# RWKV attention and a wave mixer on one core: the same tasks in another order, on other engines and banks

## The chip, the core and the metric

The kernel runs on one core of a Trainium2 chip. Five engines work side by side, each through its own list of instructions in order: TensorE (PE, with its weight loads PEld), VectorE (DVE), ScalarE (ACT), GpSimd (POOL) and SyncE (SP), which issues most transfers. The metric is the time of one execution on the device in microseconds (us): lower is better. Three runs of the kernel before gave 139.4, 140.91 and 140.97 us, a median of 140.91.

## What is computed

For batch 4, 8 heads, 768 tokens and head size 48 the first half is a linear recurrence with a decay `w` per channel and a bonus `u` for the present token; the second half mixes tokens and channels:

```python
for t in range(S):
    cur = np.einsum('bhd,bhe->bhde', u[None] * kt, vt)
    y[:, :, t] = np.einsum('bhd,bhde->bhe', rt, state + cur)
    state = w[None, :, :, None] * state + np.einsum('bhd,bhe->bhde', kt, vt)
# x = y with heads joined: (4, 768, 384)
theta = x @ w_theta
zr, zi = x * np.cos(theta), x * np.sin(theta)
u = x + einsum('ts,bsd->btd', w_tok_r, zr) + einsum('ts,bsd->btd', w_tok_i, zi)
out = u + np.maximum(u @ w_ch, 0.0)
```

Inputs and output are float32.

## The kernel before, in words

The 768 tokens of a batch are three groups of 256 tokens, so that there are twelve groups, g0 to g11. For each group `front` loads k, r and v (384 KB each, by SP, lines 436 and 442), multiplies k and r with powers of the decay into `Kw` and `Rw` (lines 551 and 553), turns both with products against an identity (line 487; the copy out of the bank into `KT` or `RT` is line 502 on ACT or 503 on DVE), forms the masked products of k and r (scores, line 601; the masked copy out is `mAT`, line 615, or an ACT copy in line 611 and a multiplication in 617 on DVE or 619 on POOL), the state sums (line 675, then `F`, `T`, `N`, `Sb`, `Sd` in lines 690 to 731), the bonus (`PD` in line 625, `diag` in 642, `dg` in 647, `yd` in 651) and the outputs (lines 751, 764, 780, or 803 and 816), which land in `x`. Then `x` is turned to `xT`, multiplied with `w_theta` (line 839), ACT takes cosine and sine (846, 850) and DVE forms `z` (854). For each batch `mixing` multiplies `z` with the turned token weights `WrT` and `WiT` (line 876, 288 products of 384 columns in all), adds x (`un`, line 889 on DVE, or 886 on ACT and 891 on POOL), turns the sum, multiplies with `w_ch` (line 906) and finishes in line 915 on DVE, or in 912 on ACT and 919 on POOL. The token weights are fetched by six transfers from POOL's queue (line 456), which also convert them, into buffers that later hold other things; each third of them is turned on PE.

Nothing in the program decides the order while it runs. All work is cut into 838 tasks, made in a fixed sequence; a table written out by hand, `ORDER`, gives the sequence in which they are issued, `WAYS` picks for each position one of the engines that the task may run on, `BANKS` gives each group of products its PSUM bank, and `IDLE` names tasks after which PE runs a few products of zeros that nobody reads (line 290, 128x512 each). Each engine then executes its instructions in this sequence, and each waits for what its data need:

```python
for seq in order:
    t = self.tasks[seq]
    way = t.ways[int(ways[seq])]
    if way[0] == PE:
        for tok in t.acq:
            self.bank_of[tok] = int(next(given))
    out = way[-1]()
    for k, n in idle.get(seq, ()):
        unread(k, n, 4)
```

So an instruction whose data are late holds up all that stands behind it on its engine.

Of the kernel before, what the change touches and what calls it, by code (L numbers as in the profile page):

```python
# [27 lines left out]


ORDER = [  # L30
# [46 lines left out]
]  # L77

WAYS = (
    "0000000000000000000000000001000000000000010100000000010000100101001000010100000000011000"  # L80
    "0010012000000000001000000000011000000000000012000000000011000000010000000000000000000000"
    "0000000010000000100100000000000100001000000111100000010010100000100000000000000010010001"
    "1000000001000000000000100100000000000000000000000000000000000000010000000000000000011010"
    "1101100001100000010110110000000000001011011000011000000000000000000000000000000011200000"
    "0000000110100001100011001001000000000001200000000000011000000111100012000100000001200000"
    "0000000000001201101100000000000120110110000110000012011011000000001200101200012120000001"
    "0110000012000000000000101200100012012001000000011000001200000000000000120000111201100000"
    "1000000012000000000000000001201101100001100000120000110000000001112011011000000000001201"
    "1011000000000111201101100001100000000110010110")

BANKS = (
    "0123456701324562704135674127530461542706524316507210431270642067520634705610761234720654"
    "1736504106713526701542765043620752163452316437021323152123756325702705217056302145701414"
    "57142542136074374036124653710465702675143067")

AFTER = []

IDLE = [
    (6, 2, 5), (29, 3, 2), (72, 5, 6), (121, 5, 3), (119, 6, 3), (102, 5, 1), (105, 2, 6),
]  # L100


# [871 lines left out]
```

## Time and profile before

| what | number |
|---|---|
| median of 3 runs | 140.91 us (139.4 to 140.97) |
| the profiled execution's own time | 140.95 us |
| its span, first to last instruction | 139.1 us |
| PE busy | 126.9 us, 91% |
| DVE busy | 114.5 us, 82% |
| ACT busy | 82.3 us, 59% |
| POOL busy | 69.9 us, 50% |
| mean granted TensorE clock | 0.988 |
| moved by DMA | 25.65 MB, 184 GB/s over the span |

In rows of the trace the first number is the start in us and the second how long it took; `L551` is the line of the program; in brackets stands how long the engine was idle just before, and what ended that. Busy time of PE is modelled from overlapping products, so two products of 0.33 us that start 0.16 us apart count once where they overlap. DVE and POOL rows include time in which an instruction has begun and makes no progress.

### The profile page before, as it was taken

Reading aid. Unit: us, or ns where it says so; the run is one execution under the profiler, and the core shown is the slowest. Engines: PE = TensorE matmul, PEld = TensorE weight load, DVE = VectorE, ACT = ScalarE, POOL = GpSimd, SP = SyncE. Lnnn points to the kernel's source line nnn. Section 1 sums busy time; section 2 is a strip of 40 time slices with the busy share of each in tenths; the row PEclk is TensorE's granted clock in tenths of the full one; section 3 lists DMA queues with packets and bytes.
Section 4 is the critical chain, followed back from the end, with each engine's and each line's share of the span. In section 5 each row is a group of like instructions: output and inputs, shape, how many; then the busy total and the mean of one; then the engine's idle time right before and its main releaser. Section 6 shows DMA issues by size and latency. Waiting matters only on the chain.

```text
span 139.1 us, 4476 instructions
## 1 busy us (share of the span) xinstructions
PE 126.9 (91%) x1867; PEld 82.9 (60%) x1867; DVE 114.5 (82%) x211; ACT 82.3 (59%) x160; POOL 69.9 (50%) x68
## 2 busy tenths in 40 slices
PE   6984998869995999999996999999999999999990
PEld 1244575547583787767774666667666665656640
DVE  7199988998989999999999999987794897473191
ACT  3862779959862339987885972686066435810110
POOL 5475629960067093099992009397956426002010
PEclk9999599999999999999999999999999999999999
DMA  4999999999999997999332088899999366365235
GB/s 103 273 261 261 266 211 289 236 249 239 246 227 238 244 188 135 212 221 170 73 114 60 5 216 179 136 265 165 172 299 224 76 184 80 68 226 169 58 125 215
DMA packets 67966, 25.65 MB, mean 184 GB/s; under 512 B 62569, under 2 KB 67946, under 8 KB 67946
## 3 DMA queue, kind: packets, MB, share of 16 engines
q1 hardware_dynamic: 65500, 22.42, 74.2%
q0 software_dynamic: 2432, 2.95, 12.3%
q8 instruction: 14, 0.23, 0.7%
q14 instruction: 6, 0.05, 0.2%
q10 hardware_dynamic: 14, 0.00, 0.0%
HBM read 20.06 MB, written 4.72 MB: 178 GB/s over the span
## 4 chain that ended last, share of the span: by engine, by line
PE 76%; DVE 17%; ACT 3%; issue 1%; DVEq 0%
PE bank L876 32%; PE bank L487 10%; PE bank L906 9%; PE bank L839 8%; PE bank L601 4%; DVE Kw L551 4%; DVE PD L625 3%; DVE mAT L615 3%; PE bank L290 3%; PE bank L675 2%; PE bank L816 2%; PE bank L751 2%; PE bank L764 1%; PE bank L642 1%; PE bank L780 1%
## 5 line engine op out<-in xcount | busy, mean ns | idle before, releaser
L876 PE MATMUL bank<-z,WrT 128*128 128x384 bf16 x144 | 46.9, 327 | 1.1 <-DVE mAT L615 1.1
L876 PE MATMUL bank<-z,WiT 128*128 128x384 bf16 x144 | 46.8, 326 | 0.0
L876 PEld LDWEIGHTS <-WiT 128*128 128x128 bf16 x144 | 14.1, 98 | 9.3 <-issue 1.4
L876 PEld LDWEIGHTS <-WrT 128*128 128x128 bf16 x144 | 14.0, 97 | 8.5 <-ACT WrT L502 0.2
L846 ACT ACTIVATE trig<-bank,pi 128x384 f16<-128x384 f32 x24 | 13.9, 585 | 8.6 <-PE bank L839 8.5
L915 DVE SCALAR_TENSOR_TENSOR fin_all<-bank,uu_all 128x384 f32<-128x384 f32 x23 | 12.3, 553 | 7.2 <-PE bank L906 6.9
L891 POOL TENSOR_TENSOR uu_all<-fin_all,x 128x384 bf16<-128x384 f32 x7 | 7.9, 1122 | 18.5 <-ACT fin_all L886 18.4
L502 ACT ACTIVATE RT<-bank 128x1024 bf16<-128x1024 bf16 x12 | 12.3, 1024 | 6.6 <-PE bank L487 6.5
L615 DVE TENSOR_TENSOR mAT<-bank,mask 128x512 bf16<-128x512 f32 x23 | 15.2, 682 | 1.0 <-PE bank L601 1.0
L611 ACT ACTIVATE mAT<-bank 128x512 bf16<-128x512 f32 x18 | 10.4, 601 | 9.2 <-PE bank L601 9.1
L839 PE MATMUL bank<-Wth,xT 128*128 128x384 bf16 x72 | 14.8, 327 | 0.2 <-DVE xT L503 0.2
L906 PE MATMUL bank<-Wch,uu_all 128*128 128x384 bf16 x72 | 14.7, 326 | 0.1
L854 DVE TENSOR_TENSOR z<-x,trig 128x1536 bf16<-128x1536 bf16 x12 | 11.7, 972 | 3.3 <-ACT trig L850 3.2
L551 POOL TENSOR_TENSOR Rw<-ld,rpow 128x768 bf16<-128x768 f32 x6 | 11.2, 1873 | 3.2 <-ACT rpow L391 2.9
L850 ACT ACTIVATE trig<-bank 128x384 f16<-128x384 f32 x24 | 11.4, 494 | 1.8 <-PE bank L839 1.6
L619 POOL TENSOR_TENSOR mAT<-mAT,mask_c 128x512 bf16<-128x512 bf16 x7 | 9.5, 1367 | 4.0 <-ACT mAT L611 4.0
L889 DVE TENSOR_TENSOR uu_all<-bank,x 128x384 bf16<-128x384 f32 x17 | 9.2, 552 | 2.7 <-PE bank L876 2.4
L290 PE MATMUL bank<-zero 128*128 128x512 bf16 x28 | 10.4, 503 | 1.1 <-DVE zero L296 1.1
L625 DVE TENSOR_TENSOR PD<-RT,KT 128x1024 bf16<-128x1024 bf16 x10 | 10.2, 1019 | 0.4 <-ACT KT L502 0.3
L886 ACT ACTIVATE fin_all<-bank 128x384 f32<-128x384 f32 x7 | 3.4, 490 | 11.8 <-PE bank L876 8.9
L601 PE MATMUL bank<-RT,KT 64*64 64x128 bf16 (+1 forms) x304 | 8.4, 219 | 1.3 <-DVE KT L503 1.3
L651 POOL TENSOR_TENSOR yd<-dg,vb 128x768 bf16<-128x768 f32 x6 | 8.9, 1476 | 1.4 <-ACT dg L647 1.3
(121 smaller groups left out, 251.1 us busy)
## 6 DMA issues: line engine op xcount, KB each, us to landing
ld<-in_r_dram SPq DMA_DIRECT2D x12, 384.0 KB, 6.8
out_dram<-fin_all SPq DMA_DIRECT2D x11, 384.0 KB, 3.0
ld<-in_k_dram SPq DMA_DIRECT2D x7, 384.0 KB, 6.2
ld<-in_v_dram SPq DMA_DIRECT2D x7, 384.0 KB, 7.1
ld<-in_k_dram SPq DMA_DIRECT2D x10, 192.0 KB, 4.1
ld<-in_v_dram SPq DMA_DIRECT2D x10, 192.0 KB, 4.9
fin_all<-in_moe_w_tok_i_dram POOLq DMA_DIRECT2D x1, 384.0 KB, 7.0
uu_all<-in_moe_w_tok_r_dram POOLq DMA_DIRECT2D x1, 384.0 KB, 7.6
```

The lines of the kernel that those rows point to most:

```text
L290: ins = [nc.tensor.matmul(bank_t[k][:, :wide * C].rearrange("p (a c) -> p a c", a=wide), zero, bc(zero, 1, wide), start=True, stop=True, s ...
L487: ins = [nc.tensor.matmul(bank16(tok)[:, i * C:(i + 1) * C], s, ident, is_transpose=True, start=(i == 0), stop=(i == n - 1)) for i, s in e ...
L502: ways = [act(n * C, lambda: nc.scalar.activation(dst, src(), Act.Copy)), dve(n * C, lambda: nc.vector.tensor_copy(dst, src()), 1.0 if pai ...
L551: return eng.tensor_mul(to.rearrange("p j h d -> p h j d")[:, :, :, :D], tokens(i), pw)
L601: ins.append(nc.tensor.matmul(to[:, hp * C:(hp + 1) * C], a, m, start=(hp == 0), stop=(hp == HP - 1), skip_group_check=True))
L615: P.add([dve(HP * C, lambda hi=hi, tk=tk, mAT=mAT, m=m: nc.vector.tensor_mul(mAT[:, hi], bank(tk[hi]).rearrange("p (h t) -> p h t", h=HP), ...
L625: return eng.tensor_mul(of[2], of[0], of[1])
L839: ins = [nc.tensor.matmul(bank(th)[:, :HD], xT[:, t, dk, :], Wth[:, dk, :], start=(dk == 0), stop=(dk == ND - 1)) for dk in range(ND)]
L846: P.add(act(HD, lambda th=th, t=t, trig=trig: nc.scalar.activation(trig[:, t, 0], bank(th)[:, :HD], Act.Sin, bias=pi2), 144), use=[th], rd ...
L876: ins.append(nc.tensor.matmul(bank(tm)[:, :HD], (WrT, WiT)[ri][:, so, to * C:(to + 1) * C], z[:, so, ri], start=(part == 0 and i == 0), st ...
L906: ins = [nc.tensor.matmul(bank(tf)[:, :HD], uT[:, t, dk, :], Wch[:, dk, :], start=(dk == 0), stop=(dk == ND - 1)) for dk in range(ND)]
L915: nc.vector.scalar_tensor_tensor(fin[:, t], bank(tf)[:, :HD], 0.0, un[:, t], op0=Alu.max, op1=Alu.add))], use=[tf], rd=[("un", j, t)],
```

## The change

Only the tables differ: `ORDER`, `WAYS`, `BANKS` and `IDLE`. The tasks, the tiles and the functions are the same. A line or two of each, and `IDLE` in full:

```diff
 ORDER = [
-    5, 1, 19, 36, 0, 15, 3, 17, 27, 7, 35, 8, 18, 9, 6, 28, 115, 4, 11, 10, 37, 14, 20, 24,
...
+    2, 1, 7, 35, 0, 5, 15, 18, 3, 9, 28, 36, 11, 19, 6, 27, 114, 4, 8, 10, 115, 12, 17, 20, 14,
...
 IDLE = [
-    (6, 2, 5), (29, 3, 2), (72, 5, 6), (121, 5, 3), (119, 6, 3), (102, 5, 1), (105, 2, 6),
+    (6, 2, 5), (74, 5, 5), (91, 5, 3), (168, 7, 2), (100, 5, 5), (146, 4, 1),
 ]
```

With the two products at the very start, which stay, there are 23 unread products instead of 28.

What changes engine, by the built programs: on DVE `Rw` 6 to 8, `Kw` of line 553 2 to 5, `KT` copies 3 to 1 and `RT` copies 0 to 1, `uu_all` copies 3 to 1, `vb` 4 to 0, `yd` 6 to 3, `N` 3 to 1, `F` copies 0 to 2, the last step of line 915 23 to 18; on POOL `Rw` 6 to 4, `Kw` of line 553 3 to 0, `vb` 0 to 5, `yd` 6 to 9, `N` 5 to 7, the sum of line 919 1 to 6; on ACT the copies of line 912 1 to 6 and `KT` 6 to 8. One more turn of `uu_all` goes over SP's queue (8 to 9), so PE turns 6 blocks fewer. The third load is k of the second group where it was r; a turn of `uu_all` now stands in SP's queue ahead of loads of later groups.

Three places. First DVE at the start: `Kw0` and `Rw0` are the scaled k and r of g0, `KT0` the copy of the turned k, `PD0` the first product of the bonus. Before:

```order
L551 TENSOR_TENSOR Kw0_107<-ld0_89,kpow_82 128x8x2x48
L365 MEMSET uw_88 128x4
L425 TENSOR_TENSOR uw_88<-bank2_63,wup_85 64x4 x2
L349 TENSOR_SCALAR mask01_72<-col_i_75,thr_76 128x128 x2
L503 COPY KT0_121<-bank4_65 128x1024
L625 TENSOR_TENSOR PD0_124<-RT0_117,KT0_121 128x1024
```

and now:

```order
L551 TENSOR_TENSOR Kw0_107<-ld0_89,kpow_82 128x8x2x48
L551 TENSOR_TENSOR Rw0_105<-ld1_90,rpow_81 128x8x2x48
L551 TENSOR_TENSOR Kw1_108<-ld3_92,kpow_82 128x8x2x48
L365 MEMSET uw_88 128x4
L410 COPY wup_85<-bank2_63 128x4
L551 TENSOR_TENSOR Rw1_106<-ld4_93,rpow_81 128x8x2x48
L625 TENSOR_TENSOR PD0_124<-RT0_117,KT0_121 128x1024
```

The masks of line 349 now stand ahead of `Kw0`, the copy of `KT0` went to ACT, and DVE scales k and r of both first groups, three of which POOL did.

Second, POOL's queue in the first stage: `Wth`, `fin_all` and `uu_all` are the first three weight transfers. Before:

```order
L698 CAST Sd0_143<-F0_131 64x4x48
L456 DMA Wth_164<-in_moe_w_theta_dram 128x3x384
L730 TENSOR_TENSOR N0_133<-T0_135,w256_86 128x192
L619 TENSOR_TENSOR mAT3_129<-mAT3_129,mask01_72 128x512
L730 TENSOR_TENSOR N1_134<-T0_135,w256_86 128x192
L456 DMA fin_all_162<-in_moe_w_tok_i_dram 128x2x768
L651 TENSOR_TENSOR yd1_151<-dg1_148,vb1_112 128x768
L456 DMA uu_all_163<-in_moe_w_tok_r_dram 128x2x768
```

and now:

```order
L619 TENSOR_TENSOR mAT0_126<-mAT0_126,mask01_72 128x512
L551 TENSOR_TENSOR Rw0_105<-ld7_96,rpow_81 128x8x2x48
L730 TENSOR_TENSOR N0_133<-T0_135,w256_86 128x192
L698 CAST Sd1_144<-N0_133 64x4x48
L651 TENSOR_TENSOR yd0_150<-dg0_147,vb0_111 128x768
L456 DMA Wth_164<-in_moe_w_theta_dram 128x3x384
L456 DMA fin_all_162<-in_moe_w_tok_i_dram 128x2x768
L456 DMA uu_all_163<-in_moe_w_tok_r_dram 128x2x768
L651 TENSOR_TENSOR yd1_151<-dg1_148,vb1_112 128x768
```

The three transfers follow each other directly, behind the bonus `yd0`.

Third, POOL's queue about the last third of the token weights (`z1` and `x2` are the buffers that they land in). Before:

```order
L698 CAST Sd1_144<-F1_132 64x4x48
L456 DMA x2_155<-in_moe_w_tok_i_dram 128x2x768
L456 DMA z1_157<-in_moe_w_tok_r_dram 128x2x768
L651 TENSOR_TENSOR yd0_150<-dg0_147,vb3_114 128x768
L891 TENSOR_TENSOR uu_all_163<-fin_all_162,x0_153 128x384
```

and now:

```order
L730 TENSOR_TENSOR N0_133<-T1_136,w256_86 128x192
L891 TENSOR_TENSOR uu_all_163<-fin_all_162,x0_153 128x384
L456 DMA z1_157<-in_moe_w_tok_r_dram 128x2x768
L456 DMA x2_155<-in_moe_w_tok_i_dram 128x2x768
L581 CAST vb4_115<-ld14_103 128x768
L551 TENSOR_TENSOR Kw1_108<-ld15_104,kpow_82 128x8x2x48
```

The two transfers now wait in the queue behind the first sum of the mixing (line 891), and a cast and a scaling of k follow them. The mask of line 353, which DVE made late, now stands on DVE ahead of `Kw3`.

More of the change, by code (lines that the diff above doesn't have):

```diff
@@ L30 @@
 ORDER = [
[46 rows of a table removed]
[46 rows of a table added]
 ]
 WAYS = (
[L80 to L89, printed above, removed]
+    "0000000000000000000000000000100000000000000100000001010010000100001010000000000012000000"
@@ new lines @@
+    "0000102000100000001000000000000000100001100000000000000100000000000000000000010000000000"
+    "0001100000000000010100000000000000002000000000000000100002000000100000000000000000020000"
+    "0011000000000000020000100100000000001001002000000110010000000000000100000000000000000120"
+    "1101100001100000000110110000000001101011011000010000000001100011000000010000000101200000"
+    "0000000010000200000000110000000000000001200000000000000000000120000012000100000001200000"
+    "0000000000111200001100000000011120110000000000000012011000000000011200000011012120001001"
@@ L91 @@
+    "0000000012000000000000011200201200011110001001000000001200000000000000120000120000011100"
+    "0000000012000000000000000001201100000000000000120110000000000001112011011000000000001201"
+    "1000000000000111201101100000000011000110010110")
 BANKS = (
-    "0123456701324562704135674127530461542706524316507210431270642067520634705610761234720654"
-    "1736504106713526701542765043620752163452316437021323152123756325702705217056302145701414"
-    "57142542136074374036124653710465702675143067")
+    "0123456701346507214706251470346273062345130761245603746513476024513607415230612734251746"
@@ L96 @@
+    "3207150417324056172436027341024357641034073564070416270462350726105767521706452314754216"
+    "4324121320567357160257260173245062415603721")
 AFTER = []
 IDLE = [
-    (6, 2, 5), (29, 3, 2), (72, 5, 6), (121, 5, 3), (119, 6, 3), (102, 5, 1), (105, 2, 6),
+    (6, 2, 5), (74, 5, 5), (91, 5, 3), (168, 7, 2), (100, 5, 5), (146, 4, 1),
 ]
```

90 rows, old and new, of the table ORDER are left out of this document.

## The prediction

> **What bounds the kernel now.** I read first the windows, to see by stages which engine is full. The columns are the stretch, its length, then busy us of PE, PEld, DVE, ACT and POOL with their instructions, the granted TensorE clock, the DMA share and GB/s.
>
> ```profile
> 13.85:17.30 3.45, 3.45 (x19) 1.90 (x17) 3.39 (x7) 2.65 (x5) 2.00 (x3) 0.51 1.26 266
> 17.30:36.20 18.90, 16.59 (x380) 11.61 (x378) 17.26 (x26) 15.86 (x31) 10.37 (x11) 1.00 1.19 242
> 44.30:80.00 35.70, 34.55 (x647) 25.17 (x645) 34.99 (x62) 26.07 (x49) 19.97 (x15) 1.00 0.75 145
> 80.00:133.20 53.20, 53.20 (x599) 34.12 (x597) 38.75 (x71) 24.91 (x55) 25.05 (x21) 1.00 0.78 165
> ```
>
> From 80 us on PE never pauses: nothing but less PE work helps there, and every lead that PE brings to 80 us shortens the run. From 44 to 80 us PE and DVE are both full (34.55 and 34.99 of 35.70). Before 44 us DVE sets the pace and PE waits for it. So I read PE's waits next: after the first stage it has two pauses of over a microsecond, at 43.71 (shown further down) and here (start, length, engine, line; in brackets the idle time before the row):
>
> ```profile
> 74.94 0.32 PE L876 MATMUL bank<-z,WrT 128*128 128x384 bf16 x1 [1.15 <-DVE mAT L615]
> ```
>
> The timeline of the start, in order of time:
>
> ```profile
> 3.41 0.48 DVE L358 TENSOR_SCALAR place<-col_i,thr 128x128 bf16<-128x128 int32 x2
> 4.29 1.12 ACT L391 ACTIVATE rpow<-z,tok_f 128x384 f32<-128x384 f32 x2
> 6.33 0.60 ACT L391 ACTIVATE kpow<-z,tok_f 128x384 f32<-128x384 f32 x1
> 6.96 1.16 DVE L551 TENSOR_TENSOR Kw<-ld,kpow 128x768 bf16<-128x768 f32 x1 [0.21 <-ACT kpow L391]
> 7.62 2.17 POOL L551 TENSOR_TENSOR Rw<-ld,rpow 128x768 bf16<-128x768 f32 x1 [0.31 <-DMA ld<-in_r_dram]
> 8.54 1.53 DVE L349 TENSOR_SCALAR mask<-col_i,thr 128x128 bf16<-128x128 int32 x2
> 10.10 1.23 DVE L503 COPY KT<-bank 128x1024 bf16<-128x1024 bf16 x1
> 10.69 1.81 POOL L551 TENSOR_TENSOR Kw<-ld,kpow 128x768 bf16<-128x768 f32 x1 [0.91 <-DMA ld<-in_k_dram]
> 11.38 0.64 PE L601 MATMUL bank<-RT,KT 64*64 64x128 bf16 x32 [1.29 <-DVE KT L503]
> ```
>
> The first scores wait for the copy of KT, and that stood on DVE behind the two masks. They took 1.53 us while POOL was scaling r; two instructions of that shape took 0.48 us before. The third and the fifth large load were awaited until 7.62 and 10.69, so a load arrives every 1.53 us.
>
> The other thing to see is what DVE loses to POOL:
>
> ```profile
> 16.20 0.93 POOL L456 DMA_DIRECT2D Wth<-in_moe_w_theta_dram  x1
> 16.64 1.15 DVE L651 TENSOR_TENSOR yd<-dg,vb 128x768 bf16<-128x768 f32 x1
> 18.89 0.68 DVE L625 TENSOR_TENSOR PD<-RT,KT 128x1024 bf16<-128x1024 bf16 x1
> 25.50 3.10 DVE L625 TENSOR_TENSOR PD<-RT,KT 128x1024 bf16<-128x1024 bf16 x1
> 26.23 1.81 POOL L551 TENSOR_TENSOR Rw<-ld,rpow 128x768 bf16<-128x768 f32 x1
> ...
> 39.89 0.72 POOL L456 DMA_DIRECT2D x<-in_moe_w_tok_i_dram  x1
> 40.52 3.13 DVE L551 TENSOR_TENSOR Kw<-ld,kpow 128x768 bf16<-128x768 f32 x1
> 40.60 0.72 POOL L456 DMA_DIRECT2D z<-in_moe_w_tok_r_dram  x1
> 41.34 1.49 POOL L651 TENSOR_TENSOR yd<-dg,vb 128x768 bf16<-128x768 f32 x1
> 43.71 0.62 PE L487 MATMUL bank<-ident,Kw 128*128 128x128 bf16 x8 [1.40 <-DVE Kw L551]
> ```
>
> The same PD takes 0.68 us at 18.89 and 3.10 at 25.50, where it ends only after POOL's train up to 28.04. Kw at 40.52 takes 3.13 us and ends after two weight transfers and a yd of POOL have gone by; the turn at 43.71 then waits 1.40 us, which is PE's longest pause in the middle.
>
> **The change, part by part.** Durations by group (busy us, mean ns):
>
> ```profile
> L502 ACT ACTIVATE RT<-bank 128x1024 bf16<-128x1024 bf16 x12 | 12.3, 1024 | 6.6 <-PE bank L487 6.5
> L551 DVE TENSOR_TENSOR Rw<-ld,rpow 128x768 bf16<-128x768 f32 x6 | 5.7, 950 | 0.3 <-DMA ld<-in_r_dram 0.3
> L615 DVE TENSOR_TENSOR mAT<-bank,mask 128x512 bf16<-128x512 f32 x23 | 15.2, 682 | 1.0 <-PE bank L601 1.0
> L617 DVE TENSOR_TENSOR mAT<-mAT,mask 128x512 bf16<-128x512 bf16 x4 | 1.7, 415 | 0.4 <-ACT mAT L611 0.4
> L915 DVE SCALAR_TENSOR_TENSOR fin_all<-bank,uu_all 128x384 f32<-128x384 f32 x23 | 12.3, 553 | 7.2 <-PE bank L906 6.9
> L651 DVE TENSOR_TENSOR yd<-dg,vb 128x768 bf16<-128x768 f32 x6 | 5.9, 985 | 0.1
> L727 DVE TENSOR_TENSOR T<-bank,F 128x192 f32<-128x192 f32 x8 | 2.7, 348 | 0.0
> L353 DVE TENSOR_SCALAR mask_c<-col_i,tok_f 128x128 bf16<-128x128 int32 x1 | 1.7, 1659 | 0.0
> ```
>
> *First scores.* ACT makes the powers for k first, so they are there at 4.29 + 1.12 = 5.41 instead of 6.93, and Kw0 starts at 5.45, 1.51 us earlier; k is now the first load. The masks are made before it. ACT has the powers for r (1.12), a fourth one (0.60) and small pieces to do until about 7.4, then copies KT and RT at 1.02 each: first scores at about 9.5 instead of 11.38. That is a gain of 1.9 us, but only if DVE can follow.
>
> *DVE up to the first z.* Set against the list before, the new one has ahead of its first z 3 more scalings (2.85), 3 more mAT (2.04), 2 more small sums (0.70), one more masking (0.42), the late mask (0.28 if free) and a copy (0.16), less two yd (1.97) and the two masks, done earlier (0.48): 4.0 us more work. Away go the collision of the masks (1.53 - 0.48 = 1.05), that of PD (3.10 - 0.68 = 2.42) and DVE's idle time from 17.30 to 36.20 (1.64). New are waits for the third and fourth load (0.8 together, from their spacing) and a wait of Kw2: POOL now has yd0 and three transfers in one train (1.49 + 0.93 + 2 x 0.72 = 3.9 us). Ahead of Kw2 DVE has 4 scalings (3.8), 6 mAT (4.1), PD (0.7), a copy of RT (1.0), 4 small sums (1.4) and trifles (0.8), 11.8 us from 5.45 on, and the 0.8 of waits: Kw2 comes at 18. I put the train's start at 16, when yd0's numbers are through PE and ACT, so that it ends at 19.9: a wait of 1.8 us (with a start at 15 it is 0.9, with 18 it is 3.9).
>
> ```profile
> 33.53 0.95 DVE L854 TENSOR_TENSOR z<-x,trig 128x1536 bf16<-128x1536 bf16 x1
> ```
>
> The first z ended at 34.48. Now: 34.48 - 1.51 + 4.0 - 1.05 - 2.42 - 1.64 + 0.8 + 1.8 = 34.5. So it is no earlier; what is earlier is the work around it. The chain of waits has the prices for PE:
>
> ```profile
> 33.04 0.67 PE bank L487 x12
> 36.34 1.95 PE bank L876 x12
> 47.40 0.17 PE bank L751 x4
> 47.57 0.50 PE bank L764 x32
> 48.07 0.33 PE bank L780 x4
> ```
>
> Before, the mixing starts at 36.34, 1.86 us after z. PE does now, ahead of it, also a state, output and bonus block (0.17 + 0.50 + 0.33) and half a set of scores (0.32) that stood behind it: 1.3 us. With the same 1.86 us after z: 36.34 + 1.3 - (34.5 + 1.86) = 1.3 us of lead. Bounds: without any new wait 2.6 more (3.9); with the old idle time and PD's collision back in other places 4.1 less (-2.8).
>
> For Kw2 there are two rows: at 16.64 a yd of DVE lost only 0.17 us (1.15 against 0.985) to a transfer being issued, at 40.52 Kw waited through two transfers. I take the second, it is the same instruction, and keep 0 to 3.9. [...]
>
> *The pause at 43.71.* DVE now scales r first, then k of g4, and the two last weight transfers stand behind the first sum of the mixing, so POOL waits there for ACT and issues nothing: -1.4 (bounds -1.4 and 0).
>
> *The pause at 74.94.* DVE was making the late mask, 1.66 us beside a long PD of POOL. It is made in the first stage now, counted there: -1.15 (0 if another instruction of DVE collides in its place).
>
> *One turn on SP instead of PE:* 6 blocks at half of 0.67: -0.35, hidden nowhere, since PE is full. Its transfer waits in SP's queue for the first sums, about 44 us, ahead of loads of g8 and g9, which were issued from 41 us on and are first used after 60: nothing, with some 10 us of cover.
>
> *Later weight transfers.*
>
> ```profile
> z<-in_moe_w_tok_r_dram POOLq DMA_DIRECT2D x1, 384.0 KB, 8.3
> ```
>
> It took 8.3 us from issue to landing. Now it is issued after the first mixing block, a copy and a sum, about 42.5, and lands at 50.8. The turns that need it stand 48 mixing products (4 x 1.95) and some 5.9 us of turns, scores and the like behind the start of the mixing at 36.4: 50.1. I take a wait of 0.7; bounds 0 and 2.4 (landing at 10 us).
>
> *Five unread products fewer, others moved:* nothing; they stand where PE has nothing else, and DVE decides there. The half clock of 13.85 to 17.30 (0.51) may come in another window; each such window costs at most half of 3.45, 1.7 us.
>
> *Afterwards,* to 80 us, DVE has to hand the lead on. It does about 4.7 us less over the run (5 last steps at 0.55, 4 vb casts and 2 turned sums priced like them, 3 yd, a copy of 1.0, together 10.0; against 5 scalings, 4.8, and 0.5 of small ones), and about 8.7 us less behind the first z. That is the cover without which the lead would be lost.
>
> Sum: -1.3 - 1.4 - 1.15 - 0.35 + 0.7 = -3.5. The profiled execution took 140.95 us (span 139.1 and 1.85 around it), the median was 140.91, so the two agree: 140.95 - 3.5 = 137.5 us.
>
> **Rivals.**
>
> *DVE keeps the lead* (22%). From 44 to 80 us it had 0.7 us free. If the work taken off it returns as collisions, only the turn and half of the second pause remain: 140.95 - 0.35 - 0.6 = 140.0. [...] Against it: the 8.7 us.
>
> *POOL's long train* (18%), the slower end. Behind the first sum POOL now runs two transfers, a cast, a scaling of k (1.8), more sums, Wch, another scaling and a PD with few waits. Each two-input instruction of DVE caught behind such a train loses what Kw lost, 3.13 - 0.95 = 2.2 us. One or two are in the forecast's slack; from the second on PE waits, and three on the path cost 6.6: 140.95 - 3.5 + 6.6 = 144.1.
>
> *No collision at all at the start* (10%): Kw2 is let in at once and the loads are in time: -2.6, 134.9.
>
> That the tables don't do what they say is excluded by the built program's lists.
>
> **How the numbers follow.** Forecast 50%, the rivals 22, 18 and 10. The forecast's own range is 135.5 to 139.5. The range reaches from 134.6 to 143.5: below it lies half of the fastest case, above it some two thirds of the slowest. A measurement of this kernel tells about 2% from no change, 138.1 and 143.7: of the forecast 0.36 lies below the first, with the fastest case 0.46; 0.16 is slower; 0.38 between.
>
> **What would show it.** Right: first scores at 9 to 10 us; Kw of g2 long (over 1.5 us) about 18 to 21; the mixing from about 36.5 with the g3 outputs done; no pause of PE over 1 us between 40 and 80; PE full from 80 to about 130. Wrong: if the first scores come after 11, the step on ACT's powers fails; if Kw2 takes 0.95, the collision; if PE waits for DVE in several rows between 45 and 75, the cover; if PE's wait for turned weights is over 2 us, the transfers.

## The result, and the profile after

| | kernel before | changed kernel |
|---|---|---|
| median of 4 runs each | 140.16 us (139.2 to 140.97) | 146.15 us (145.13 to 147.07) |
| profiled execution, its span | 140.95 us, 139.1 us | 146.42 us, 144.7 us |
| mean granted TensorE clock | 0.988 | 0.976 |

The ratio is 1.043, with a 95% interval from 1.032 to 1.054: slower, where 137.5 us had been forecast. Medians, here and below, are of all executions, while ratios leave out those over 1.5% above the fastest of their kernel, so the two can differ a little. The later comparisons below have the kernel before beside them again, 41 runs with medians of 139.45 to 139.57 us: the profiled execution on which the sum was built, 140.95 us at a clock of 0.988, was a long one.

The windows of the changed kernel (stretch, length, busy us of PE, PEld, DVE, ACT and POOL, granted clock, DMA share, GB/s):

```profile
17.30:36.20 18.90, 18.16 (x410) 12.53 (x409) 17.92 (x34) 17.73 (x38) 11.06 (x11) 1.00 1.15 230
36.20:44.30 8.10, 8.10 (x132) 5.75 (x131) 7.61 (x11) 4.61 (x8) 4.58 (x5) 1.00 0.96 231
50.00:60.00 10.00, 4.31 (x105) 3.70 (x103) 9.94 (x8) 3.50 (x7) 6.99 (x5) 0.86 0.73 119
60.00:70.00 10.00, 10.00 (x146) 6.43 (x144) 6.33 (x12) 5.68 (x12) 1.04 (x2) 0.80 0.20 15
80.00:133.20 53.20, 50.95 (x626) 32.61 (x625) 38.36 (x64) 29.55 (x62) 28.06 (x25) 1.00 0.93 167
```

Up to 44 us PE does more than before (18.16 against 16.59, then 8.10 of 8.10), as hoped. From 50 to 60 it works 4.31 us of 10 while DVE is "busy" all the time, and the clock falls. Half clock for a time t within 10 us lowers the mean by t/20: 0.86 is 2.8 us, so from 57.2 on, and 0.80 is 4.0 us, so to 64.0; taken over just that stretch, 57.2 to 64.0, the granted clock is 0.50. In the stretch 60 to 70 us the transfers nearly stand still (0.20, 15 GB/s), and after 80 us they are denser than before (0.93 against 0.78).

The timeline of the same kernel at the places that the prediction named:

```profile
8.42 2.34 PE L290 MATMUL bank<-zero 128*128 128x512 bf16 x5
10.69 0.64 PE L601 MATMUL bank<-RT,KT 64*64 64x128 bf16 x16
...
18.57 0.93 POOL L456 DMA_DIRECT2D Wth<-in_moe_w_theta_dram  x1
18.84 0.95 DVE L551 TENSOR_TENSOR Kw<-ld,kpow 128x768 bf16<-128x768 f32 x1
31.15 0.94 DVE L854 TENSOR_TENSOR z<-x,trig 128x1536 bf16<-128x1536 bf16 x1
34.41 0.34 PE L876 MATMUL bank<-z,WrT 128*128 128x384 bf16 x1
41.33 0.72 POOL L456 DMA_DIRECT2D x<-in_moe_w_tok_i_dram  x1
42.49 2.73 DVE L625 TENSOR_TENSOR PD<-RT,KT 128x1024 bf16<-128x1024 bf16 x1
45.87 0.50 PE L487 MATMUL bank<-ident,uu_all 128*128 128x128 bf16 x6 [0.67 <-DVE mAT L615]
...
49.77 0.80 POOL L456 DMA_DIRECT2D Wch<-in_moe_w_ch_dram  x1
50.50 7.33 DVE L551 TENSOR_TENSOR Rw<-ld,rpow 128x768 bf16<-128x768 f32 x1
50.60 1.82 POOL L551 TENSOR_TENSOR Kw<-ld,kpow 128x768 bf16<-128x768 f32 x1
52.38 2.11 POOL L625 TENSOR_TENSOR PD<-RT,KT 128x1024 bf16<-128x1024 bf16 x1
54.45 1.79 POOL L551 TENSOR_TENSOR Rw<-ld,rpow 128x768 bf16<-128x768 f32 x1
56.20 0.81 POOL L581 CAST vb<-ld 128x768 bf16<-128x768 f32 x1
57.75 0.55 DVE L790 CAST x<-bank 128x384 bf16<-128x384 f32 x1
58.35 1.01 PE L487 MATMUL bank<-ident,Rw 128*128 128x128 bf16 x8 [5.69 <-DVE x L790]
59.79 0.53 PE L876 MATMUL bank<-z,WrT 128*128 128x384 bf16 x1
64.58 0.33 PE L876 MATMUL bank<-z,WrT 128*128 128x384 bf16 x1
67.51 1.31 SPq L493 DMA_TRANSPOSE uu_all<-uu_all  x1
...
98.36 0.62 PE L601 MATMUL bank<-RT,KT 64*128 64x128 bf16 x16 [0.54 <-DMA KT<-Kw]
103.28 1.15 PE L839 MATMUL bank<-Wth,xT 128*128 128x384 bf16 x6 [1.51 <-DMA xT<-x]
```

Read it from 50.50 on. DVE's scaling of r of g6, 0.95 us elsewhere, takes 7.33: it ends at 57.83, when POOL's four instructions, one straight behind the other, are done (56.20 + 0.81 = 57.01) and another 0.82 us has passed. PE stands still for 5.69 us, since the turn that it has next needs this scaling, and its bank is read by the copy `x` behind it on DVE. Then products take 0.53 us instead of 0.33 until 64: 58.35 to 64.0 at half speed is another 2.8 us. SP's queue waits with the transposed sums until 67.51, three loads behind them; at 98 and 103 us PE waits for transposed tiles. The list of waits says the same in two rows (total, times, longest):

```profile
PE bank L487 <- DVE x L790: 5.7, 1, 5.7
PEld L487 <- DVE Rw L551: 5.4, 1, 5.4
```

5.7 + 2.8 + 2.0 is more than the whole distance to the kernel before; what the change brought lies underneath.

### The profile page after: what moved, and what is told of

It is laid out like the page before. It is cut to its first block, busy times and chain, and to the rows that moved or that the text cites. A ratio compares the mean times of both kernels' runs of the same rounds, so it can differ in the third digit from the quotient of the medians.

```text
span 144.7 us, 4479 instructions
## 1 busy us (share of the span) xinstructions
PE 129.8 (90%) x1856; PEld 84.4 (58%) x1856; DVE 113.7 (79%) x203; ACT 84.7 (59%) x167; POOL 69.1 (48%) x73
## 4 chain that ended last, share of the span: by engine, by line
PE 56%; DMA 14%; DVE 11%; issue 8%; ACT 7%; POOL 2%; DVEq 0%; POOLq 0%; ACTq 0%
PE bank L876 26%; PE bank L487 11%; DMA xT<-x 6%; DMA fin_all<-in_moe_w_tok_r_dram 5%; PE bank L906 5%; PE bank L839 3%; DMA KT<-Kw 3%; PE bank L601 2%; DVE PD L625 2%; PE bank L290 2%; DVE mAT L615 2%; ACT KT L502 1%; DVE Kw L551 1%; PE bank L311 1%; PE bank L675 1%
## 5 line engine op out<-in xcount | busy, mean ns | idle before, releaser
L876 PE MATMUL bank<-z,WrT 128*128 128x384 bf16 x144 | 48.0, 334 | 0.0
L876 PE MATMUL bank<-z,WiT 128*128 128x384 bf16 x144 | 47.8, 333 | 0.0
L651 POOL TENSOR_TENSOR yd<-dg,vb 128x768 bf16<-128x768 f32 x9 | 13.9, 1545 | 10.0 <-ACT dg L647 8.0
L891 POOL TENSOR_TENSOR uu_all<-fin_all,x 128x384 bf16<-128x384 f32 x7 | 6.4, 915 | 18.8 <-ACT fin_all L886 18.8
L615 DVE TENSOR_TENSOR mAT<-bank,mask 128x512 bf16<-128x512 f32 x21 | 14.1, 681 | 1.2 <-PE bank L601 1.1
L551 DVE TENSOR_TENSOR Rw<-ld,rpow 128x768 bf16<-128x768 f32 x8 | 14.2, 1769 | 1.0 <-DMA ld<-in_r_dram 0.9
L487 PE MATMUL bank<-ident,Rw 128*128 128x128 bf16 x96 | 8.6, 242 | 5.7 <-DVE x L790 5.7
L915 DVE SCALAR_TENSOR_TENSOR fin_all<-bank,uu_all 128x384 f32<-128x384 f32 x18 | 9.8, 551 | 3.1 <-PE bank L906 3.0
L487 PEld LDWEIGHTS <-Rw 128*128 128x128 bf16 x96 | 6.9, 108 | 7.1 <-DVE Rw L551 5.4
L919 POOL TENSOR_TENSOR fin_all<-fin_all,uu_all 128x384 f32<-128x384 f32 x6 | 5.9, 977 | 10.0 <-ACT fin_all L912 9.8
```

Of the source, the lines that this page charges most:

```text
L487: ins = [nc.tensor.matmul(bank16(tok)[:, i * C:(i + 1) * C], s, ident, is_transpose=True, start=(i == 0), stop=(i == n - 1)) for i, s in e ...
L551: return eng.tensor_mul(to.rearrange("p j h d -> p h j d")[:, :, :, :D], tokens(i), pw)
L615: P.add([dve(HP * C, lambda hi=hi, tk=tk, mAT=mAT, m=m: nc.vector.tensor_mul(mAT[:, hi], bank(tk[hi]).rearrange("p (h t) -> p h t", h=HP), ...
L651: return eng.tensor_mul(yd.rearrange("p a b d -> p (a b) d"), wide(dg, D), vb.rearrange("p a b d -> p (a b) d"))
L876: ins.append(nc.tensor.matmul(bank(tm)[:, :HD], (WrT, WiT)[ri][:, so, to * C:(to + 1) * C], z[:, so, ri], start=(part == 0 and i == 0), st ...
```

## The experiments

Theory 1: the one held scaling, with the half clock that follows. Theory 2: DVE and PE have no slack from 44 to 80 us, so that a wait taken away returns elsewhere. Theory 3: SP's queue, on which loads stand behind transpositions that wait. In `AFTER` a pair (a, b) makes task b wait for task a; 400 is DVE's scaling of r of g6, 399 POOL's scaling of k of g6, 317 POOL's PD of g5. Ratios are to the kernel before on the same chip.

**1. The scaling first.**

```diff
-AFTER = []
+AFTER = [(400, 399)]
```

> The changed kernel, with one wait added: POOL's scaling of k of g6 (the first instruction of its train at 50.60 us) waits for DVE's scaling of r of g6 (50.50 us, which took 7.33 us there). Theory 1, the train: DVE's scaling was held out until POOL's four instructions had gone by; first on its pair, it takes 0.95 us, PE's wait of 5.7 us goes and with it the half clock after it (some 2.8 us): 146.2 - 8.5 = 137.7 us, range 136 to 140. Theory 2, DVE and PE have no slack here: the wait moves to the next instruction caught behind the same train, and the time stays above 144 us. Theory 3, SP's queue (a transposition that waits for its sums stands ahead of three loads, and the loads come too late from 98 us on): the waits of 1.5 and 0.5 us at 103 and 98 us stay, and the time does not fall below 142 us.

Measured: 137.96 us, ratio 0.988 (0.985 to 0.991). Its timeline:

```profile
45.47 0.49 PE L487 MATMUL bank<-ident,uu_all 128*128 128x128 bf16 x6 [0.67 <-DVE mAT L615]
50.10 0.94 DVE L551 TENSOR_TENSOR Rw<-ld,rpow 128x768 bf16<-128x768 f32 x1
51.13 1.81 POOL L551 TENSOR_TENSOR Kw<-ld,kpow 128x768 bf16<-128x768 f32 x1 [0.96 <-DVE Rw L551]
52.91 2.13 POOL L625 TENSOR_TENSOR PD<-RT,KT 128x1024 bf16<-128x1024 bf16 x1
54.76 1.10 DVE L854 TENSOR_TENSOR z<-x,trig 128x1536 bf16<-128x1536 bf16 x1
55.01 2.53 POOL L551 TENSOR_TENSOR Rw<-ld,rpow 128x768 bf16<-128x768 f32 x1
94.13 1.15 PE L839 MATMUL bank<-Wth,xT 128*128 128x384 bf16 x6 [1.36 <-DMA xT<-x]
```

The scaling takes 0.94 us, POOL waits 0.96, PE has no wait above 0.7 us between 45 and 80. (What the expectation calls the scaling's pair no run shows; the rows show the order and these times.) One wait of a microsecond on POOL gives back 8.2 us (by the ratios 7.7), 0.3 less than worked out. Theory 2 falls. Theory 3's wait (94.13) does remain, but the time falls far below the 142 us that it allowed.

**2. The train broken behind its first instruction.**

```diff
-AFTER = []
+AFTER = [(400, 317)]
```

> The changed kernel, with one wait added in another place: the second instruction of POOL's train (the long PD of g5, at 52.38 us) waits for DVE's scaling of r of g6. POOL's scaling of k still goes first. Theory 1, the train: DVE is held for that one instruction alone, about 2.8 us instead of 7.33, PE waits about 1.2 us and keeps its clock: 146.2 - 4.5 - 2.8 = 138.9 us, range 137 to 141.5. Theory 2 (no slack): above 144 us. [...]

Measured: 139.07 us, ratio 0.993 (0.989 to 0.997). Its timeline:

```profile
50.23 2.75 DVE L551 TENSOR_TENSOR Rw<-ld,rpow 128x768 bf16<-128x768 f32 x1
50.33 1.83 POOL L551 TENSOR_TENSOR Kw<-ld,kpow 128x768 bf16<-128x768 f32 x1
53.13 2.12 POOL L625 TENSOR_TENSOR PD<-RT,KT 128x1024 bf16<-128x1024 bf16 x1 [0.97 <-DVE Rw L551]
53.50 0.61 PE L487 MATMUL bank<-ident,Rw 128*128 128x128 bf16 x8 [1.11 <-DVE x L790]
```

The same collision with a train of one instruction: 2.75 us (0.10 until POOL's row begins, 1.83 for it, 0.82 behind it) instead of 7.33, a wait of 1.11 us, no half clock (granted 1.00 from 50 to 70 us). So in this place the hold lasts until POOL's train pauses: in the changed kernel DVE, waiting since 50.50, was not let in at any of the three changes from one instruction of the train to the next.

It is not so everywhere. In the first experiment's trace DVE's `z` begins at 54.76, while POOL's PD runs (52.91 to 55.04). It is let in at the change and takes 1.10 us, and POOL's scaling, which stood ready straight behind PD, waits in its place: 2.53 us, where the same scaling took 1.79 in the changed kernel. The four places in the two kernels where a two-input instruction of DVE was passed over by an instruction of POOL that began later (25.50 and 40.52 in the kernel before, 42.49 and 50.50 in the changed one) have in common that POOL issued a transfer directly ahead of its train. But a yd of DVE in the kernel before (16.64, 1.15 us) also began beside such an issue and was not passed over by POOL's next instruction. No run moves the transfer, so what makes POOL keep its turn stays open. Which row begins first does not settle it: the scaling at 50.50 begins 0.10 us ahead of POOL's and waits for all four (7.33 us).

**3. The pause filled with unread products, wrong bank.** 24 products into bank 1 behind task 387:

```diff
-    (6, 2, 5), (74, 5, 5), (91, 5, 3), (168, 7, 2), (100, 5, 5), (146, 4, 1),
+    (6, 2, 5), (74, 5, 5), (91, 5, 3), (168, 7, 2), (100, 5, 5), (146, 4, 1), (387, 1, 24),
```

> The changed kernel, with 24 more unread products of zeros on PE behind the turn of the sums at 52.17 us, in the pause (24 x 0.21 = 5.1 us of the 5.69). DVE's scaling stays held for some 7.3 us. Theory 1: the half clock that followed the pause (57.1 to 64.0 us) is gone, which gives 2.8 us: 143.4 us, range 142 to 144.5. Were the clock the larger share of the loss, 141 us or less. If the products don't keep the clock, or their own time is in the way, 146 us or more.

Measured: 151.65 us, ratio 1.078 (1.072 to 1.083). A PE row of it:

```profile
59.20 1.01 PE L290 MATMUL bank<-zero 128*128 128x512 bf16 x2 [5.69 <-DVE x L790]
```

The products waited as well: bank 1 is the one that the held DVE still had to read. They ran after the pause, most of them at half clock (0.81 granted from 60 to 70 us), and cost 5.5 us. The experiment says nothing on what the half clock costs; it shows only that unread products, too, wait for a bank whose reader is held.

**4. Three loads ahead of the transposed sums.**

```diff
-    406, 407, 321, 421, 416, 319, 349, 350, 411, 412, 280, 423, 409, 392, 323, 424, 414, 451,
+    406, 407, 321, 421, 416, 319, 490, 489, 488, 349, 350, 411, 412, 280, 423, 409, 392, 323,
```

(490, 489 and 488 are taken out further down.)

> The changed kernel, with three loads (r of g9, two halves of k) ahead of the turned sums on SP's queue instead of behind them. Theory 1, the train: the pause of 5.7 us and the half clock stay; only the late waits of PE (1.5 us at 103, 0.5 at 98) can go: 144 to 146.5 us. Theory 3, SP's queue: most of the loss comes from the loads that stood still from 54 to 69 us: 142 us or less.

Measured: 145.08 us, ratio 1.039 (1.034 to 1.044). The scaling is held for 7.33 us as before and PE waits 5.70; of the late waits only 0.51 us at 102.41 is left. So SP's queue was worth 1 us at most of the changed kernel's time (the intervals overlap), as a consequence of the pause, and theory 3 as the main cause falls.

**5. The pause filled, in a free bank.**

```diff
-    (6, 2, 5), (74, 5, 5), (91, 5, 3), (168, 7, 2), (100, 5, 5), (146, 4, 1),
+    (6, 2, 5), (74, 5, 5), (91, 5, 3), (168, 7, 2), (100, 5, 5), (146, 4, 1), (48, 0, 22),
```

> The changed kernel, with 22 unread products in PE's pause of 5.7 us, this time in a bank that nobody behind DVE's held instruction reads (the one that ACT empties at about 53.3 us). DVE stays held for 7.3 us. Theory 1 (the pause and then the half clock after it): PE idles only some 0.6 us, the stretch from 57.1 to 64.0 us runs at full clock, and the time falls by 2.8 us: 143.4 us, range 142 to 145. If the clock had no share, 146 us.

Measured: 142.99 us, ratio 1.025 (1.023 to 1.028). Its timeline:

```profile
50.12 7.34 DVE L551 TENSOR_TENSOR Rw<-ld,rpow 128x768 bf16<-128x768 f32 x1
52.80 4.91 PE L290 MATMUL bank<-zero 128*128 128x512 bf16 x22 [0.52 <-ACT WiT L502]
57.99 0.61 PE L487 MATMUL bank<-ident,Rw 128*128 128x128 bf16 x8 [0.28 <-DVE x L790]
58.78 0.33 PE L876 MATMUL bank<-z,WrT 128*128 128x384 bf16 x1
```

Nothing is faster on DVE, yet 3.2 us are back (by the ratios 2.4): the products behind the pause take 0.33 us at once. So some 3 of the 8.2 us are the half clock with what it entailed (PE's later waits for transposed tiles fell too, from 2.3 to 1.3 us), and the other 5 are the standing still and what it entailed. The granted clock of this execution is 1.00 from 44.3 to 80 us, where the changed kernel's is 0.50 from 57.2 to 64.0. PE's wait of 1.11 us in the second experiment brought no half clock, the one of 5.69 us did; how long a pause must be for that, and what ends the 6.8 us, no run shows.

**6. What held Kw in the kernel before?** The prediction took two transfers for it. Here POOL's yd of g3 (226) waits for DVE's scaling of k of g4 (253), in the kernel before:

```diff
-AFTER = []
+AFTER = [(253, 226)]
```

> The kernel before, with one wait added: POOL's yd at 41.34 us waits for DVE's scaling of k of g4 (40.52 us, 3.13 us there). If two transfers being issued on POOL hold a DVE instruction with two inputs, as the prediction chose, the scaling still ends only behind them, at about 42.3 us (1.7 us long). [...] Either way PE's pause of 1.40 us at 43.71 goes: 139.5 - 1.4 = 138.1 us, range 137.7 to 139.5 (the latter if the lead is lost again to DVE before 80 us).

Measured: 137.93 us, ratio 0.990 (0.988 to 0.992). Its timeline:

```profile
38.19 0.72 POOL L456 DMA_DIRECT2D x<-in_moe_w_tok_i_dram  x1
38.82 0.95 DVE L551 TENSOR_TENSOR Kw<-ld,kpow 128x768 bf16<-128x768 f32 x1
38.90 0.72 POOL L456 DMA_DIRECT2D z<-in_moe_w_tok_r_dram  x1
39.93 1.47 POOL L651 TENSOR_TENSOR yd<-dg,vb 128x768 bf16<-128x768 f32 x1 [0.31 <-DVE Kw L551]
```

The same transfers lie beside the scaling at the same distance (0.08 us after its start), and it takes 0.95 us instead of 3.13. The transfers alone do not hold it; yd did. What stays open is how yd, whose row begins 0.8 us after that of the scaling, got ahead of it in the kernel before. In the changed kernel POOL's Kw at 50.60 also came a moment after DVE's start at 50.50, behind a transfer.

This trace shows one thing more. Up to 38 us its program is the kernel before. That kernel's profiled execution was at half clock from 13.85 to 17.30 (0.51), and its first product of the mixing is this:

```profile
36.18 0.33 PE L876 MATMUL bank<-z,WrT 128*128 128x384 bf16 x1
```

The execution with the added wait kept its clock there (1.00) and began the mixing 1.70 us earlier:

```profile
12.80:17.30 4.50, 3.82 (x74) 2.68 (x74) 4.44 (x9) 3.58 (x7) 2.06 (x3) 1.00 1.27 264
34.48 0.33 PE L876 MATMUL bank<-z,WrT 128*128 128x384 bf16 x1
```

So the 1.4 us by which the profiled execution is longer than the median of 139.5 were lost in that window.

**7. Two more held instructions released,** on top of the first experiment: DVE's PD of g4 (270) ahead of POOL's scaling of k of g5 (300), and a masking (267) ahead of a yd (273):

```diff
-    303, 369, 304, 299, 273, 378, 305, 267, 379, 380, 248, 40, 69, 245, 42, 381, 41, 282, 400,
+    303, 369, 304, 299, 267, 273, 378, 305, 379, 380, 248, 40, 69, 245, 42, 381, 41, 282, 400,
...
-AFTER = []
+AFTER = [(400, 399), (270, 300), (267, 273)]
```

> The kernel of the first experiment (138.0 us) with two more waits on POOL, so that its instructions don't hold DVE's PD of g4 (2.73 us at 42.08, 0.68 when free) and one masking (1.52 us at 48.19, 0.43 when free): DVE gets 3.1 us back. Theory 1 (held instructions cost where PE waits behind them): PE's pause of 0.67 us at 45.47 goes and little else, 137.3 us, range 136.5 to 138. If DVE as a whole bounds this stage, up to 3 us less: 135 us.

Measured: 136.97 us, ratio 0.978 (0.974 to 0.982). Its timeline:

```profile
8.12 1.24 PE L290 MATMUL bank<-zero 128*128 128x512 bf16 x5
9.69 0.42 PE L601 MATMUL bank<-RT,KT 64*64 64x128 bf16 x16 [0.33 <-ACT RT L502]
43.09 0.97 DVE L625 TENSOR_TENSOR PD<-RT,KT 128x1024 bf16<-128x1024 bf16 x1
48.01 0.42 DVE L617 TENSOR_TENSOR mAT<-mAT,mask 128x512 bf16<-128x512 bf16 x1
94.36 1.15 PE L839 MATMUL bank<-Wth,xT 128*128 128x384 bf16 x6 [1.34 <-DMA xT<-x]
```

PD takes 0.97 us instead of 2.73 and the masking 0.42 instead of 1.52, PE's wait at 45.47 is gone, and the time falls by 1.0 us (by the ratios 1.4), not by the 2.9 that DVE got back. DVE now has idle time instead (0.49 us before 44.55, 0.80 before 49.23): what it is spared counts only where PE waits for it.

**8. Fewer unread products at the start,** on top of the first experiment:

```diff
-    (6, 2, 5), (74, 5, 5), (91, 5, 3), (168, 7, 2), (100, 5, 5), (146, 4, 1),
+    (6, 2, 5), (74, 5, 2), (91, 5, 3), (168, 7, 2), (100, 5, 5), (146, 4, 1),
```

> The kernel of the first experiment (138.0 us) with 2 unread products instead of 5 behind the first turn of r. If those five, which PE works off until 10.7 us, are what delays the first scores (ready at 9.7), the scores begin at 9.7 us and the time falls by up to 1.0 us: 137.0. If DVE sets the pace up to the first z, the earlier scores bring nothing: 138.0 us. If the clock falls to half because PE idles there, a loss of up to 1.7 us: 139.7.

Measured: 137.56 us, ratio 0.984 (0.980 to 0.988), which overlaps with that of the first. The first scores came at 10.05 us. In the seventh experiment's profile, with all five products, they came at 9.69, since the products took 1.24 us there and 2.34 in the changed kernel's profile. When PE becomes fast at the start differs between executions; the number of products is worth less than can be told here.

**9 and 10. The seventh with the loads of the fourth, and with the fewer products of the eighth.** The tenth has both edits, the ninth only the first (with `AFTER` as in the seventh):

```diff
-    406, 407, 321, 421, 416, 319, 349, 350, 411, 412, 280, 423, 409, 392, 323, 424, 414, 451,
+    406, 407, 321, 421, 416, 319, 490, 489, 488, 349, 350, 411, 412, 280, 423, 409, 392, 323,
...
-    (6, 2, 5), (74, 5, 5), (91, 5, 3), (168, 7, 2), (100, 5, 5), (146, 4, 1),
+    (6, 2, 5), (74, 5, 2), (91, 5, 3), (168, 7, 2), (100, 5, 5), (146, 4, 1),
```

> The kernel of the seventh experiment (137.0 us, 0.978 of the kernel before) with the three loads ahead of the turned sums on SP's queue, as in the fourth. Theory 3 in its small form (the loads that stand behind the waiting transposition crowd the transfers later, where PE waits 1.3 us at 94 and 0.6 us at 90 for transposed tiles): those two waits shrink, 135.5 to 136.5 us. If those waits come from the transpositions' own place on SP's queue, nothing: 137.0 us.

> The kernel of the ninth experiment with 2 unread products instead of 5 behind the first turn of r, as in the eighth. In the eighth this moved the time by 0.4 us with an interval as wide; if the five products only cost where they fall into a stretch at half clock, the same here: 0 to 0.6 us below the ninth. If the fewer products bring on more half clock at the start, 0 to 1 us above it.

Measured: 137.16 us, ratio 0.983 (0.979 to 0.988), for the ninth. Its late PE rows:

```profile
89.43 0.62 PE L601 MATMUL bank<-RT,KT 64*128 64x128 bf16 x16 [0.59 <-DMA KT<-Kw]
93.90 1.15 PE L839 MATMUL bank<-Wth,xT 128*128 128x384 bf16 x6 [1.06 <-DMA xT<-x]
```

The late waits stay, so without the pause it is not the order of these loads. For the tenth the median is 136.94 us. Its ratio, 0.969 (0.964 to 0.974), rests on two executions (134.71 and 135.87 us); three more took 136.8 to 137.5 us and one 241 us, for which no cause is known, so nothing is claimed from it. The best that is well measured is the seventh, 2.2% below the kernel before; the ninth overlaps with it.

## Why the prediction was wrong, point by point

- **First scores at 9.5 us:** 10.69 in the changed kernel's profile, 9.69 in the seventh experiment's. The chain over ACT and DVE was right; that the unread products cost "nothing" was not, when they run slowly (2.34 us), though it decides little.
- **Kw of g2 held for 1.8 us:** wrong. The row at 18.84 has 0.95 us beside a transfer being issued. Of two rows that disagreed I chose the one whose instruction was the same, and read the wrong neighbour in it: the sixth experiment shows that yd held it, not the transfers. The first z was ready at 32.1 us instead of 34.5, but 1.7 us of that are the half clock of the execution that the sum started from: in the sixth experiment's trace, with the old order and the full clock, z was ready at 32.8.
- **The lead at the mixing:** the first product stands at 34.41. Set against 36.18 in the profiled execution before, it is 1.8 us earlier, but that execution had lost 1.7 us to its half clock; set against 34.48, it is 0.1 us earlier, with 1.3 us of work done ahead of it that stood behind it before. That is about 1.4 us, where 1.3 was forecast. The term is right in size and partly by luck: the wait of Kw2 in it did not come, and even so z was ready only 0.7 us before the 32.8 of that trace.
- **The pause at 43.71 and the one at 74.94:** both gone, as forecast; the late mask took 0.28 us in its new place. The first is confirmed in the kernel before itself: without it 1.5 us less (1.40 forecast). In its place a small one of 0.67 came.
- **Later weight transfers, 0.7:** no wait. **The turn on SP, "nothing, with some 10 us of cover":** the cover was there only as long as PE kept its schedule; with the pause the transposition waited to 67.51 and the loads behind it cost up to 1 us (fourth experiment).
- **"Afterwards, to 80 us, DVE has to hand the lead on":** this is the step that failed. It compared sums of busy time (8.7 us less for DVE) and let them cover the collisions. A sum covers no single wait: DVE was busy for 9.94 us of the ten from 50 to 60, of which 6.4 were one instruction being held. The sum had no term for that wait, and PE stood still behind it for 5.69 us.
- **The rival that came true** is POOL's long train, forecast at 18% and 144.1 us. Its mechanism and its place are right, its size is not: it priced each catch at 2.2 us, from a hold by one instruction, and needed three. There was one of 7.33 - 0.95 = 6.4 us on the path, because this hold lasted through the whole train, and the prediction had listed that train itself (a scaling of k, another scaling, a PD). The half clock was priced at 1.7 us at most for a window; after a pause of 5.7 us it cost 2.8 as worked out from the windows, 2.4 to 3.2 as measured with what it entailed.
- **The sum without the catch:** the first experiment gave 137.96 us where 137.5 stood. That the two are close is luck: the sum started from an execution 1.4 us longer than the median of 139.5, and took off 3.5 where 1.5 came. Its gains (a lead of 1.4, the two pauses and the turn) add up to 4.3 and fit what the traces show, though the second pause and the turn were not tested singly. What it had put at nothing are new waits of PE, 2.4 us in the first experiment's trace (0.67 for DVE, 1.36 and 0.41 for transposed tiles), in place of the 0.7 for turned weights.

## What to carry to other kernels

Before moving two-input work between DVE and POOL, write down for each such DVE instruction which POOL instructions can stand ready around it without a wait between them, above all behind a transfer that POOL issues: there the price of a collision was the rest of the train (6.4 us), elsewhere the rest of one instruction (in the first experiment 1.52 us instead of 0.42 for the masking at 48.19, 1.10 instead of 0.95 for `z` at 54.76). One wait on POOL, placed so that DVE's instruction goes first, cost a microsecond here and saved all of it. A balance of busy time tells whether a stage has room, not whether an instruction on the path will be late. The one long pause of PE here was paid about one and a half times (5.7 us and some 2.8 at half clock). And a sum should start from the median execution, not from the one that was profiled, above all where the profile shows a half clock that other executions may not have.

## What the runs showed of the hardware that was not expected

- A DVE instruction with two inputs in SBUF was held through four POOL instructions in a row (7.33 us in place of 0.95), through one in the second experiment (2.75), and through none when POOL had to wait for it (0.94). In all three POOL had issued a transfer directly ahead.
- Away from such issues DVE was let in between two instructions of POOL that stood ready one behind the other (1.10 us at 54.76 in the first experiment), and POOL's second one waited (2.53 us).
- Transfers being issued on POOL held no such instruction: 0.95 us at 38.82 (sixth experiment) and at 18.84.
- The short one-input cast of DVE from SBUF to SBUF (`Sd`, 0.26 us free at 58.79) took 1.06 us beside the train in the first experiment and 1.42 in the second.
